# Global blocks as three ordinary steps with weights, placed first in a batch, and the experts' schedule moved

## The chip, the core and the metric

The kernel runs on one core of a Trainium2 chip. The metric is device time in microseconds of one execution; lower is better. The core has TensorE (matmuls; PE in the profile, PEld its weight loads), VectorE (DVE), ScalarE (ACT), GpSimd (POOL) and SyncE (SP, which here only issues transfers). Each runs its own instructions in program order and waits on the others by semaphores.

## What is computed

Block-sparse attention (4 batches, 8 heads, 768 tokens, head size 64, blocks of 32 tokens), then a small expert network on the 128 tokens of each batch with the highest gate score. Cut to what matters:

```python
mask = abs(blk_i - blk_j) <= 1
mask |= (blk_i == 0) | (blk_j == 0) | (blk_i == 23) | (blk_j == 23)
for qb in range(24):
    for kb in sampled_blocks[qb]: mask[qb block, kb block] = True   # 3 drawn key blocks
attn = softmax(where(mask, q @ k.T / 8, -1e9)); x = attn @ v
scores = x @ w_gate                                # per token, x: 768 x 512
top = the 128 tokens of a batch with the highest scores
out[top] = x[top] + sigmoid(scores[top]) * (relu(x[top] @ w1) @ w2)   # w1: 512 x 1024
```

Query blocks 0 and 23 see all 24 key blocks ("global" below); the other 22 see at most eight.

## The kernel before

Tokens are worked in pairs of query blocks, units 0 to 11 of a batch. Unit 0 is the global pair, blocks 0 and 23; the other 11 units are ordinary. Heads are split in two groups g of four (partition halves), and in `ph`, `p2`.

An ordinary unit is one step. `unit_scores` (270) puts the scores of the shared keys and of the gathered ones (`kr`) in two PSUM tiles of the pool `ps_s` (four banks); `maxima` (313) reduces them on VectorE, two instructions; `exps` (328) makes the probabilities on ScalarE, four instructions; `turn` (344) transposes them on TensorE, eight transposes in two banks of `ps_t`, the first evicted by ScalarE and the second by VectorE (`pc`, `pt`); `out_unit` (377) multiplies by v (`vs` shared, `vr` gathered) into the one bank of `ps_o`; `norm` (394) divides by the sums and sends the rows out; `gate` (412) makes the tokens' gate scores in `sps[b]`. `gather` (245) fetches a unit's v rows by indirect DMA on GpSimd and copies its key blocks there, `gather_act` (261) the rest on ScalarE, both three steps ahead.

The global pair takes two steps, `ph` 0 and 1, which stand sixth and seventh among the 13 steps of a batch (`GLOB = 5`, 591). `glob_scores` (297) fills four tiles of 384 columns a step, in two halves; `maxima` takes four reductions and joins the halves; so all 24 key blocks of a row have one maximum. `out_glob` (365) accumulates both steps in one bank, with v of all blocks in `vg` (one 1.6 MB tile, loaded by `load_vg`, 95).

The main loop (640) is written out by hand: iteration s issues prefetches (605), the gather of step s + 3, `norm` and `gate` of s - 1, `turn` of s, `exps` of s + 1, scores of s + 2, the output of s and the maxima of s + 2. Loads are issued on SP in that order. Expert weights: `w_load` (222) and `w_split` (227), one tile of 256 KB in each of steps 1 to 16, split two steps later by ScalarE and VectorE in a high and a low part.

`route` (428) lays out a batch's expert as a plan of (offset, place, piece) counted from the end of its attention (`at`, 421; `run`, 424): `row`, `row_out` and `spread` bring the 768 scores to all partitions over DRAM (for the last batch `on_chip` (451) does it by a matmul with ones); `columns` (463) turns them into columns; six `rank` pieces (483) count on VectorE how many scores are larger; `select` (492), `chosen` (499) and `fetch` (504) fetch the 128 rows by indirect DMA; `xt`, `w1_mm`, `relu`, `ht`, `w2_mm` are the expert (its inputs split in two parts by `split`, 520), `put` (568) the last sum and the scatter. The expert's tiles all come from the one bank of `ps_m` (`mid`, 524). A plan (577 to 585) is 28 steps long: batch 2's runs past the attention, and batch 3's lies behind it.

```python
    plan = [(0, "b", row), (1, "a", row_out), (2, "a", spread)]
plan += [(4, "b", columns), (5, "a", columns_out)]
plan += [(5 + t, "c", lambda t=t: rank(t)) for t in range(6)]
plan += [(11, "a", select), (11, "b", chosen), (12, "a", fetch), (14, "b", xt), (15, "a", xt_out)]
plan += [(15 + i, "b", lambda i=i: w1_mm(0, 4 * i, 4 * i + 4)) for i in range(3)]
plan += [(18, "a", lambda: relu(0)), (18, "b", lambda: ht(0)), (19, "a", lambda: ht_out(0))]
plan += [(19 + i, "b", lambda i=i: w1_mm(1, 4 * i, 4 * i + 4)) for i in range(3)]
plan += [(22, "a", lambda: relu(1)), (22, "b", lambda: ht(1)), (23, "a", lambda: ht_out(1))]
plan += [(23 + i, "b", lambda i=i: w2_mm(6 * i, 6 * i + 6)) for i in range(4)]
```

## Time and profile before

| | us |
|---|---|
| three runs | 355.46, 349.16, 346.52 |
| median | 349.16 |
| the profiled execution | 350.02 |
| its span, first to last instruction | 348.20 |

Times are device time. The profile records one execution; "busy" is time in which an engine worked, "idle before" the pause ahead of an instruction with what ended it. In the program's names, s and gs are scores, mx and gm maxima, pr and gpr probabilities, pt and pc their transposes in PSUM and in SBUF, o and go outputs, h, ht and y the expert's tiles, sb the scores on all partitions, cj the ranks' counts, xe the fetched rows. All operations go through one helper, so every line is L67 and the tiles tell them apart.

### The profile page before, as it was taken

Reading aid. Unit: us, or ns where it says so; the run is one execution under the profiler, and the core shown is the slowest. Engines: PE = TensorE matmul, PEld = TensorE weight load, DVE = VectorE, ACT = ScalarE, POOL = GpSimd, SP = SyncE. Lnnn points to the kernel's source line nnn. Section 1 sums busy time; section 2 is a strip of 40 time slices with the busy share of each in tenths; the row PEclk is TensorE's granted clock in tenths of the full one; section 3 lists DMA queues with packets and bytes.
Section 4 is the critical chain, followed back from the end, with each engine's and each line's share of the span. In section 5 each row is a group of like instructions: output and inputs, shape, how many; then the busy total and the mean of one; then the engine's idle time right before and its main releaser. Section 6 shows DMA issues by size and latency. Waiting matters only on the chain.

```text
span 348.2 us, 13754 instructions
## 1 busy us (share of the span) xinstructions
PE 276.8 (79%) x5508; PEld 206.0 (59%) x5508; DVE 234.7 (67%) x697; ACT 155.6 (45%) x400; POOL 165.9 (48%) x356
## 2 busy tenths in 40 slices
PE   3378789872977878799899988998999968776772
PEld 3266457662754666577567766775677756554551
DVE  4457768774877799997647998677479964761000
ACT  1145658644655665355445553454455531110110
POOL 3688832771770657588426575684165211001001
PEclk9999999997999999899999999999999999887678
DMA  5799886998898749889837597975254312001000
GB/s 212 217 306 332 260 287 184 290 339 236 233 308 266 240 143 311 258 225 293 248 119 235 156 344 214 278 216 167 71 148 118 102 24 86 0 0 60 0 0 30
DMA packets 32038, 65.78 MB, mean 189 GB/s; under 512 B 5736, under 2 KB 12136, under 8 KB 31976
## 3 DMA queue, kind: packets, MB, share of 16 engines
q1 hardware_dynamic: 24296, 39.39, 36.8%
q0 software_dynamic: 7680, 25.53, 24.4%
q8 instruction: 43, 0.70, 0.8%
q14 instruction: 19, 0.16, 0.1%
HBM read 57.55 MB, written 7.35 MB: 186 GB/s over the span
## 4 chain that ended last, share of the span: by engine, by line
PE 44%; DVE 20%; issue 15%; DMA 11%; ACT 5%; POOL 2%; SPq 1%; POOLq 1%; ACTq 0%; DVEq 0%
PE o L67 11%; PE s L67 9%; PE pt L67 7%; PE h L67 5%; DVE mx L67 5%; DMA w<-w 5%; PE y L67 4%; PE gs L67 4%; DVE cj L67 3%; DVE gm L67 3%; ACT pr L67 3%; PE go L67 3%; DMA k<-kt 2%; DVE w_l L67 1%; DVE pc L67 1%
## 5 line engine op out<-in xcount | busy, mean ns | idle before, releaser
L67 POOL DMA_INDIRECT vr<-vt,vidx x88 | 88.0, 1001 | 74.3 <-PE o L67 28.3
L67 DVE TENSOR_REDUCE mx<-s 128x2 f32<-128x512 f32 x88 | 56.5, 682 | 23.7 <-PE s L67 22.2
L67 ACT ACTIVATE pr<-s,mx 128x256 f32<-128x256 f32 x176 | 69.4, 486 | 3.2 <-DVE mx L67 3.2
L67 POOL COPY kr<-k 128x128 f32 (+1 forms) x220 | 63.1, 330 | 4.9 <-PE s L67 4.6
L67 ACT COPY pc<-pt 128x512 f32<-128x512 f32 x44 | 25.7, 585 | 64.5 <-PE pt L67 64.5
L67 PE MATMUL pt<-ident,pr 128*128 128x128 f32 x352 | 50.4, 286 | 1.3 <-DVE ts L67 0.6
L67 PEld LDWEIGHTS pt<-ident,pr 128*128 128x128 f32 x352 | 40.6, 146 | 8.8 <-issue 3.0
L67 PE MATMUL o<-vs,pc 128*64 128x65 f32 x704 | 30.9, 229 | 18.4 <-ACT pr L67 8.6
L67 PEld LDWEIGHTS o<-vs,pc 128*64 128x64 f32 x704 | 25.1, 139 | 31.0 <-ACT pr L67 14.2
L67 PE MATMUL s<-k,q 64*64 64x128 f32 x704 | 31.8, 296 | 9.4 <-DMA vs<-vt 8.1
L67 PE MATMUL s<-kr,q 64*32 64x128 f32 x1408 | 32.0, 286 | 7.0 <-POOL kr L67 3.6
L67 PE MATMUL o<-vr,pc 128*32 128x65 f32 x1408 | 31.0, 225 | 3.3 <-issue 3.3
L67 DVE COPY pc<-pt 128x512 f32<-128x512 f32 x44 | 30.0, 683 | 3.1 <-PE pt L67 2.7
L67 PEld LDWEIGHTS s<-k,q 64*64 64x64 f32 x704 | 20.2, 139 | 17.5 <-DVE q L67 8.4
L67 PEld LDWEIGHTS s<-kr,q 64*32 64x32 f32 x1408 | 19.1, 110 | 16.0 <-issue 11.1
L67 DVE TENSOR_REDUCE gm<-gs 128x1 f32<-128x384 f32 x32 | 16.3, 551 | 16.9 <-PE gs L67 16.9
L67 PE MATMUL y<-w_h,h_hl 128*128 128x512 f32 x64 | 25.1, 451 | 3.0 <-DVE h_hl L67 2.8
L67 ACT COPY kr<-k 128x128 f32 x88 | 22.9, 326 | 10.3 <-DMA vs<-vt 9.8
L67 PEld LDWEIGHTS o<-vr,pc 128*32 128x32 f32 x1408 | 23.1, 111 | 7.0 <-issue 3.9
L67 DVE TENSOR_SCALAR_CACHE_REDUCE cj<-sb,sc 128x128 bf16<-128x128 f32 (+5 forms) x44 | 26.7, 641 | 0.1
L67 PE MATMUL h<-w_h,x_hl 128*128 128x512 f32 x64 | 22.1, 475 | 5.8 <-DVE h_hl L67 3.0
L67 DVE CUSTOM_DVE_ANT_0 j<-x,wg_i 128x256 f32<-128x256 f32 x48 | 22.6, 470 | 0.0
(102 smaller groups left out, 342.2 us busy)
## 6 DMA issues: line engine op xcount, KB each, us to landing
q<-qt SPq DMA_DIRECT2D x16, 384.0 KB
k<-kt SPq DMA_DIRECT2D x16, 384.0 KB
...
vr<-vt,vidx POOLq DMA_INDIRECT x88
```

The lines of the kernel that those rows point to most:

```text
L67: i = getattr(self.engine, name)(*args, **kw)
```

## The change

A batch has 14 steps: the global pair first, as three steps c = 0, 1, 2 of eight key blocks each, then the 11 units. A global step has the form of a unit: two score tiles, two reductions, four exps, eight transposes, 16 output matmuls. Each has its own maxima. `glob_keep` copies the first two outputs (with their sums) out of PSUM on VectorE; `glob_weights` makes the weights exp(own maximum - common maximum); `glob_join` weighs and adds the first two on GpSimd; `glob_last` weighs the third and adds on VectorE; `norm` then divides as before. `vg` comes in three tiles, q's first chunk and the opening's k in parts, in a new order. The maxima of step 0 follow the index arithmetic on VectorE; no gather stands ahead of step 0. Weight tiles are loaded in two of three steps from step 4 on.

In a step in which a piece stands at place "z" (ranks, mostly), ScalarE evicts both transposes. Batches 0 and 1: plan of 24 steps; batch 2 ranks two tiles a step and ends after 19. The last batch: scores of units 0 to 7 are summed four steps before the end of attention, and the first four rank tiles are counted against them in the last two steps; the other third follows behind (`rk` has a fourth column). Its expert tiles, except y, take banks of `ps_s`, and its pieces are interleaved: w1's second half around `ht(0)`, w2's first six around `ht(1)`.

```diff
-WARM = 26
+WARM = 40
...
-    def load_vg(b):
-
-        vg = vgs[b] = inp.tile([P, NB // 4, VR], F32, tag="vg", name=f"vg{b}", bufs=1)
...
+    def load_vg(b, c):
+
+        vg = vgs[b, c] = inp.tile([P, 2, VR], F32, tag="vg", name=f"vg{b}_{c}", bufs=3)
+        r = rows_of(b, 1 + 8 * c)
+        if c < 2:
+            sp.dma_start(vg, vt[r:r + 256].rearrange("(m p) c -> p m c", p=P))
+            return
+        sp.dma_start(vg[:, 0], vt[r:r + 128])
...
-    load_q(0, 0)
-    for c in range(4):
-        load_k(0, 6 * c, 6 * c + 6)
+    load_q(0, 0, 0, 1)
+    load_k(0, 0, 8)
+    load_k(0, 8, 16)
+    load_vg(0, 0)
+    load_k(0, 16, 24)
+    load_q(0, 0, 1, 3)
+    load_vg(0, 1)
     load_vs(0, 1)
-    load_vs(0, 2)
+    load_q(0, 1)
...
+    scale_q(0, 0, 0, 1)
...
-    def glob_scores(b, ph, h):
-        for g in range(G):
-            st[b, "g", ph, g, h] = ps_s.tile([P, 512], F32, tag="s", name=f"gs{b}_{ph}_{g}_{h}")
-        for p2 in range(2):
...
+    def glob_scores(b, c):
+
+        t = [st.setdefault((b, "g", c, g), ps_s.tile([P, 2, 8, BLK], F32, tag="s", name=f"gs{b}_{c}_{g}"))
+             for g in range(G)]
+        for ph in range(2):
+            for p2 in range(2):
+                p = 2 * p2 + ph
+                for g in range(G):
+                    rows = slice(64 * g, 64 * g + 64)
+                    pe.matmul(t[g][64 * p2:64 * p2 + 64, ph], qs[b, 0][rows, 0, p],
+                              ks[b][rows, 8 * c:8 * c + 8, p * BLK:(p + 1) * BLK],
+                              start=ph == 0, stop=ph == 1, tile_position=(64 * g, 64 * p2), skip_group_check=True)
...
+            b, _, c = t
+            if c == 0:
+                gms[b] = small.tile([P, 3, G, 2], F32, tag="gm", name=f"gm{b}", bufs=2)
+            mx = mxs[t] = gms[b][:, c]
...
+        for g in range(G):
+            pr = prs[(*t, g)] = work.tile([P, 512], F32, tag="pr", name=f"pr{tag_of(t)}_{g}", bufs=5)
+            s = st.pop((*t, g)).rearrange("p h k c -> p h (k c)")
+            for ph in range(2):
+                act.activation(pr[:, 256 * ph:256 * ph + 256], s[:, ph], AF.Exp, bias=mx[:, g, ph:ph + 1])
...
+    def turn(t, both):
+
+        pr = [prs.pop((*t, g)) for g in range(G)]
...
-            if c % 8 == 0:
+                c = 256 * (i % 2) + 128 * n
+                pe.transpose(pm[:, i], pr[i // 2][:, c:c + 128], ident)
+            pt = work.tile([P, 4, P], F32, tag="pt", name=f"pc{tag_of(t)}_{n}", bufs=4)
+            if n == 0 or both:
                 act.copy(pt, pm)
             else:
                 vec.tensor_copy(pt, pm)
...
+
+    def glob_weights(b):
+        gm, gw = gms[b], gws.setdefault(b, small.tile([P, 3, NP], F32, tag="gw", name=f"gw{b}", bufs=2))
+        gm = gm.rearrange("p c g h -> p c (g h)")
+        m = small.tile([P, NP], F32, tag="gx", name=f"gx{b}", bufs=2)
+        vec.tensor_tensor(m, gm[:, 0], gm[:, 1], ALU.min)
+        vec.tensor_tensor(m, m, gm[:, 2], ALU.min)
+        vec.tensor_tensor(gw, m.unsqueeze(1).broadcast_to([P, 3, NP]), gm, ALU.subtract)
+        act.activation(gw, gw, AF.Exp)
+
+    def glob_keep(b, c):
+        og = ogs[b, c] = work.tile([P, NP, VW], F32, tag="og", name=f"og{b}_{c}", bufs=2)
+        vec.tensor_copy(og, os_.pop((b, "g", c)))
+
+    def weight(b, c):
+        return gws[b][:, c].unsqueeze(2).broadcast_to([P, NP, VW])
+
+    def glob_join(b):
+        for c in range(2):
+            pool.tensor_tensor(ogs[b, c], ogs[b, c], weight(b, c), ALU.mult)
+        pool.tensor_tensor(ogs[b, 0], ogs[b, 0], ogs[b, 1], ALU.add)
+
+    def glob_last(b):
+        og = ogs.pop((b, 1))
+        vec.tensor_tensor(og, os_.pop((b, "g", 2)), weight(b, 2), ALU.mult)
+        vec.tensor_tensor(og, og, ogs.pop((b, 0)), ALU.add)
+        os_[b, 0] = og
+
+    def out_glob(b, c):
+        o = os_[b, "g", c] = ps_o.tile([P, NP, VW], F32, tag="o", name=f"go{b}_{c}")
+        pt, vg = pts.pop((b, "g", c)), vgs.pop((b, c))
+        for n in range(2):
...
+                    h = p2 * 4 + i
+                    pe.matmul(o[64 * p2:64 * p2 + 64, i], pt[n][:, i, 64 * p2:64 * p2 + 64],
+                              vg[:, n, h * VW:(h + 1) * VW], start=n == 0 and i == 0, stop=n == 1 and i == NP - 1,
+                              tile_position=(0, 64 * p2), skip_group_check=True)
...
-        def on_chip():
-            r = rout.tile([P, FF], F32, tag="hs", name=f"r{b}")[:, 0:S]
-            R["sb"] = rout.tile([P, S], F32, tag="sb", name=f"sb{b}")
...
+        def masked(u0, u1):
+            if "sb" not in R:
+                R["sb"] = rout.tile([P, S], F32, tag="sb", name=f"sb{b}")
+            r = R["r"] = rout.tile([P, 8, 2 * BLK], F32, tag="r", name=f"r{u0}")
+            vec.tensor_tensor(r[:, :u1 - u0], sps[b][:, u0:u1].unsqueeze(2).broadcast_to([P, u1 - u0, 2 * BLK]),
+                              d64.unsqueeze(1).broadcast_to([P, u1 - u0, 2 * BLK]), ALU.mult)
+
+        def sums(u0, u1):
+            R["sbp"] = ps_t.tile([P, 512], F32, tag="t", name=f"sbp{u0}")
+            pe.matmul(R["sbp"][:, :64 * (u1 - u0)], ones, R["r"][:, :u1 - u0].rearrange("p u c -> p (u c)"),
+                      start=True, stop=True)
+
+        def sums_out(u0, u1):
+            act.copy(R["sb"][:, 64 * u0:64 * u1], R["sbp"][:, :64 * (u1 - u0)])
+
+        def columns(t0=0, t1=6):
+            R["scp"] = small_t([P, 6, BLK], f"scp{t0}_")
+            for t in range(t0, t1):
                 pe.transpose(R["scp"][:, t], R["sb"][0:BLK, t * P:(t + 1) * P], ident[0:BLK, 0:BLK])
...
-        def columns_out():
...
+        def columns_out(t0=0, t1=6):
+            if t0 == 0:
+                R["sc"] = rout.tile([P, 6], F32, tag="sc", name=f"sc{b}", bufs=2)
+                R["rk"] = rout.tile([P, 6, 4], F32, tag="rk", name=f"rk{b}", bufs=2)
+                vec.memset(R["rk"], 0.0)
+            vec.tensor_copy(R["sc"][:, t0:t1], R["scp"][:, t0:t1, 0])
...
+        def parts():
+            sc, tb = R["sc"], rout.tile([P, 6, 5], BF16, tag="tb", name=f"tb{b}", bufs=2)
+            R["tb"] = tb
...
-        def rank(t):
-            sb, s, n = R["sb"], R["sc"][:, t:t + 1], t * P
...
+        def rank(t, c0=0, c1=S):
+            sb, s, n, rk = R["sb"], R["sc"][:, t:t + 1], t * P, R["rk"]
+            junk = rout.tile([P, S], BF16, tag="cj", name=f"cj{b}_{t}_{c0}")
+            if c0 < n:
+                vec.tensor_scalar(junk[:, c0:n], sb[:, c0:n], s, 0.0, ALU.is_ge, ALU.add, accum_out=rk[:, t, 0:1])
+            n1 = max(n, c0)
+            i = 3 if c0 > n else 1
+            vec.tensor_scalar(junk[:, n1:c1], sb[:, n1:c1], s, 0.0, ALU.is_gt, ALU.add, accum_out=rk[:, t, i:i + 1])
+            if c0 <= n:
+                vec.scalar_tensor_tensor(junk[:, n:n + P], sb[:, n:n + P], s, before, ALU.is_equal, ALU.mult,
+                                         accum_out=rk[:, t, 2:3])
...
         def mid(name):
+            if last and name != "y":
+                return ps_s.tile([P, 512], F32, tag="s", name=f"{name}{b}")
             return ps_m.tile([P, 512], F32, tag="m", name=f"{name}{b}")
...
+                R["h1", c] = mid(f"h1_{c}")
...
-                pe.matmul(R["h1"], *parts[n], start=n == 0, stop=n == 11)
+                pe.matmul(R["h1", c], *parts[n], start=n == 0, stop=n == 11)
...
         if last:
-            plan = [(0, "b", on_chip)]
+            early = 8
+            plan += [(-4, "z", lambda: masked(0, early)), (-3, "m", lambda: sums(0, early)),
+                     (-3, "z", lambda: sums_out(0, early)), (-2, "m", lambda: columns(0, 4)),
+                     (-2, "z", lambda: columns_out(0, 4))]
+            plan += [(-2 + t // 2, "z", lambda t=t: rank(t, 0, 64 * early)) for t in range(4)]
+            plan += [(0, "z", lambda: masked(early, NU)), (0, "z", lambda: sums(early, NU)),
+                     (0, "z", lambda: sums_out(early, NU)), (1, "n", lambda: columns(4, 6))]
+            plan += [(1, "z", lambda t=t: rank(t, 64 * early, S)) for t in range(4)]
+            plan += [(2, "z", lambda: columns_out(4, 6)), (2, "z", parts), (2, "z", lambda: rank(4)),
+                     (2, "z", lambda: rank(5)), (3, "z", select), (4, "n", chosen), (5, "a", fetch),
+                     (6, "n", xt), (7, "a", xt_out)]
+            w1s(7, 0, 0, 12)
+            plan += [(8, "a", lambda: relu(0))]
+            w1s(8, 1, 0, 8)
+            plan += [(8, "n", lambda: ht(0)), (9, "a", lambda: ht_out(0))]
+            w1s(9, 1, 8, 12)
+            plan += [(10, "a", lambda: relu(1))]
+            w2s(10, 0, 6)
+            plan += [(10, "n", lambda: ht(1)), (11, "a", lambda: ht_out(1))]
+            w2s(11, 6, 24)
+            plan += [(12, "a", put)]
...
-            plan = [(0, "b", row), (1, "a", row_out), (2, "a", spread)]
-        plan += [(4, "b", columns), (5, "a", columns_out)]
-        plan += [(5 + t, "c", lambda t=t: rank(t)) for t in range(6)]
-        plan += [(11, "a", select), (11, "b", chosen), (12, "a", fetch), (14, "b", xt), (15, "a", xt_out)]
-        plan += [(15 + i, "b", lambda i=i: w1_mm(0, 4 * i, 4 * i + 4)) for i in range(3)]
-        plan += [(18, "a", lambda: relu(0)), (18, "b", lambda: ht(0)), (19, "a", lambda: ht_out(0))]
-        plan += [(19 + i, "b", lambda i=i: w1_mm(1, 4 * i, 4 * i + 4)) for i in range(3)]
-        plan += [(22, "a", lambda: relu(1)), (22, "b", lambda: ht(1)), (23, "a", lambda: ht_out(1))]
-        plan += [(23 + i, "b", lambda i=i: w2_mm(6 * i, 6 * i + 6)) for i in range(4)]
-        plan += [(27, "a", put)]
+            fast = b == B - 2
+            plan += [(0, "n", row), (1, "a", row_out), (2, "a", spread), (3, "n", columns), (4, "a", columns_out),
+                     (4, "a", parts)]
+            plan += [(4 + (t // 2 if fast else t), "z", lambda t=t: rank(t)) for t in range(6)]
+            o = 7 if fast else 10
+            plan += [(o, "a", select), (o, "n", chosen), (o + 1, "a", fetch), (o + 2, "n", xt), (o + 3, "a", xt_out)]
+            o += 3
...
+            w1s(o + 1, 0, 6, 12)
+            plan += [(o + 2, "a", lambda: relu(0)), (o + 2, "n", lambda: ht(0)), (o + 3, "a", lambda: ht_out(0))]
+            w1s(o + 3, 1, 0, 6)
+            w1s(o + 4, 1, 6, 12)
+            plan += [(o + 5, "a", lambda: relu(1)), (o + 5, "n", lambda: ht(1)), (o + 6, "a", lambda: ht_out(1))]
+            if fast:
+                w2s(o + 6, 0, 12)
+                w2s(o + 7, 12, 24)
+                plan += [(o + 9, "z", put)]
+            else:
+                for i in range(4):
+                    w2s(o + 6 + i, 6 * i, 6 * i + 6)
+                plan += [(o + 10, "a", put)]
...
-    GLOB = 5
     steps = []
     for b in range(B):
-        units = [(b, u) for u in range(1, NU)]
-        steps += units[:GLOB] + [(b, "g", 0), (b, "g", 1)] + units[GLOB:]
-    n, per = len(steps), NU + 1
...
         b, i = steps[s][0], s % per
-        t = unit_at(s)
+        t = unit_at(s + 1)
         if t:
-            k = inner.index(t) + 3
+            k = inner.index(t) + 2
             if k < len(inner):
                 load_vs(*inner[k])
-        for c, load, scale in ((2, 0, 3), (3, 5, 7), (4, 8, 10), (5, 9, 12)):
-            bq, cq = b + c // 4, c % 4
-            if bq < B and i == load:
-                load_q(bq, cq)
-            if bq < B and i == scale:
-                scale_q(bq, cq)
+        for c, load, scale in ((3, 4, 8), (4, 6, 10), (5, 9, 13), (6, 12, 16)):
+            if i == load and b + c // 4 < B:
+                load_q(b + c // 4, c % 4)
+            bs = b if scale < per else b - 1
+            if i == scale % per and bs >= 0 and bs + c // 4 < B:
+                scale_q(bs + c // 4, c % 4)
         if b + 1 < B:
...
-            if 4 <= i < 8:
-                load_k(b + 1, 6 * (i - 4), 6 * (i - 4) + 6)
-            if i == 9:
-                load_vg(b + 1)
-        if s == 1:
...
+            if i in (5, 7, 8, 10):
+                j = (5, 7, 8, 10).index(i)
+                load_k(b + 1, 6 * j, 6 * j + 6)
+            if i >= 11:
+                load_vg(b + 1, i - 11)
+
+    load_vg(0, 2)
+    load_vs(0, 2)
+    load_q(0, 2)
+    for s in range(2):
+        scores(steps[s])
+        if s:
+            exps(steps[0])
+        maxima(steps[s])
+    route(B - 1, n)
     for s in range(n + 1):
...
+            b, i = steps[s - 1][0], (s - 1) % per
+            done = None if i < 2 else (b, 0) if i == 2 else steps[s - 1]
+            if i < 2:
+                glob_keep(b, i)
+            if i == 0:
+                glob_weights(b)
+            if i == 1:
+                glob_join(b)
+            if i == 2:
+                glob_last(b)
+            if done:
+                norm(*done)
         if s < n:
...
+            turn(steps[s], (s, "z") in due)
...
+            if s + 2 < n:
+                scores(steps[s + 2])
+            run(s, "m")
+            t = steps[s]
             if t[1] == "g":
                 out_glob(t[0], t[2])
             else:
                 out_unit(*t)
...
+            run(s, "n")
             if s + 2 < n:
                 maxima(steps[s + 2])
-            run(s, "c")
-        if 3 <= s:
-            w_split(s - 3)
-        if 1 <= s < 1 + len(ws):
-            w_load(s - 1)
-        if s < n and (s + 1) % per == 0:
+            if s == 0:
+                scale_q(0, 0, 1, 3)
+            if s in (2, 4):
+                scale_q(0, s // 2)
+            run(s, "z")
+        if 6 <= s and (s - 6) % 3 < 2:
+            w_split((s - 6) // 3 * 2 + (s - 6) % 3)
+        if 4 <= s and (s - 4) % 3 < 2:
+            w_load((s - 4) // 3 * 2 + (s - 4) % 3)
+        if s < n and (s + 1) % per == 0 and s + 1 < n:
             route(s // per, s + 1)
     for s, where in sorted(due):
         run(s, where)
```

## Rows read from the trace of the kernel before

**Rows 1.** Stage table: stretch, length, busy PE, PEld, DVE, ACT, POOL, clock, DMA, GB/s.
```profile
0.00:20.13 20.13, 7.30 (x123) 5.50 (x123) 7.65 (x35) 4.55 (x12) 10.63 (x35) 1.00 0.74 223
20.13:87.41 67.28, 52.52 (x1304) 39.43 (x1297) 47.70 (x117) 38.50 (x99) 40.64 (x84) 0.96 0.89 278
87.41:152.59 65.18, 52.72 (x1314) 39.45 (x1310) 55.73 (x165) 36.61 (x96) 39.24 (x83) 0.96 0.81 250
152.59:221.21 68.62, 62.64 (x1372) 46.88 (x1366) 54.86 (x165) 35.75 (x95) 40.74 (x85) 1.00 0.76 232
221.21:287.85 66.64, 60.33 (x1270) 45.09 (x1268) 49.40 (x153) 33.12 (x85) 29.62 (x62) 1.00 0.48 135
165.80:190.45 24.65, 21.97 (x383) 15.10 (x382) 15.13 (x41) 12.60 (x30) 10.48 (x26) 1.00 0.68 206
...
287.85:312.65 24.80, 19.56 (x80) 14.34 (x81) 15.45 (x57) 4.03 (x8) 2.02 (x6) 0.86 0.08 24
...
318.33:341.45 23.12, 18.82 (x56) 13.44 (x56) 1.38 (x2) 2.37 (x4) 0.00 (x0) 0.72 0.00 0
```

**Rows 2.** Chain that ended last, start and us: a unit step, y.
```profile
264.97 0.87 PE pt L67 x8
265.84 1.19 PE s L67 x48
267.04 1.21 PE o L67 x48
268.25 1.13 PE h L67 x4
...
282.91 1.60 PE y L67 x6
```

**Rows 3.** Timeline of ScalarE, batch 0: start, us, instruction, [idle before].
```profile
82.67 0.62 ACT L67 CAST w_h<-w 128x512 fp32r<-128x512 f32 x1 [7.41 <-DMA w<-w]
```

**Rows 4.** Timeline of TensorE, the global steps of batch 2.
```profile
173.25 1.34 PE L67 MATMUL gs<-k,q 64*64 64x384 f32 x8 [1.44 <-ACT gpr L67]
...
179.49 1.25 PE L67 MATMUL pt_g<-ident,gpr 128*128 128x128 f32 x8 [0.68 <-ACT pc_g L67]
```

**Rows 5.** Timeline of VectorE, the opening.
```profile
5.20 0.20 DVE L67 CAST rb<-rb_i 128x72 f32<-128x72 int32 x1 [2.36 <-DMA rb_i<-blocks]
...
11.12 0.55 DVE L67 TENSOR_SCALAR q<-q 128x768 f32<-128x768 f32 x1
...
16.56 1.29 DVE L67 TENSOR_REDUCE mx<-s 128x2 f32<-128x512 f32 x2 [4.89 <-PE s L67]
```

**Rows 6.** Instruction groups: busy us, mean ns, idle before.
```profile
L67 DVE TENSOR_REDUCE mx<-s 128x2 f32<-128x512 f32 x88 | 56.5, 682 | 23.7 <-PE s L67 22.2 <-PE o L67 1.4
...
L67 DVE COPY pc<-pt 128x512 f32<-128x512 f32 x44 | 30.0, 683 | 3.1 <-PE pt L67 2.7
...
L67 DVE TENSOR_TENSOR x<-o,z 128x256 f32<-128x256 f32 x44 | 18.7, 424 | 1.9 <-DVE z L67 0.4
L67 POOL COPY kr<-k 128x256 f32<-128x256 f32 x44 | 17.5, 397 | 0.0
...
L67 DVE TENSOR_SCALAR_CACHE_REDUCE cj<-sb,sc 128x128 bf16<-128x128 f32 (+5 forms) x44 | 26.7, 641 | 0.1
```

**Rows 7.** The gate product: its tile (least, median, most ns) and the timelines.
```profile
L67 DVE CUSTOM_DVE_ANT_0 j<-x,wg_i x48: 413/416/840, 27.2 to 288.8; 128x256 f32<-128x256 f32 x48
...
104.00 0.84 DVE L67 CUSTOM_DVE_ANT_0 j<-x,wg_i 128x256 f32<-128x256 f32 x1
...
103.56 1.54 POOL L67 COPY kr<-k 128x128 f32 x5
```

**Rows 8.** Chain and TensorE's timeline, the end.
```profile
312.65 3.46 DMA xe<-out,it
...
318.34 2.08 PE L67 MATMUL h<-w_h,x_hl 128*128 128x512 f32 x4 [1.46 <-DVE x_hl L67]
```

**Rows 9.** Chain that ended last, after the stall of batch 0.
```profile
85.32 2.16 PE o L67 x48
```

165 lines of the change are left out of this document (38 added, 127 removed).

## The prediction

> **What bounds the kernel now.** I read the stage table first, cut at the starts of the batches' first steps and at the events of the end [rows 1]. The reader is to see three regimes. Batches 2 and 3 are TensorE: 62.64 of 68.62 us and 60.33 of 66.64 us busy at clock 1.00. Batches 0 and 1 are not: 52.5 us of work in 67.3 and 65.2 us, with DMA shares of 0.89 and 0.81. The last 60 us (287.85 to 348.20) are one dependent chain at a clock of 0.86 and then 0.72. The chain of waits then gives the unit step at full clock [rows 2]: eight transposes 0.87, scores 1.19, output 1.21, so 3.3 us, and an expert piece on top (four h matmuls 1.13, six y matmuls 1.60). ScalarE's timeline shows the biggest stall of batch 0: its cast of a weight tile, which stands in order ahead of the probabilities, waited 7.41 us for a load [rows 3]. TensorE's timeline shows the stall of the global blocks [rows 4]: the scores of one global step take all four score banks, so the next ones wait 1.44 us for the exps, and transposes wait 0.68 us for an eviction. That stretch loses 24.65 - 21.97 = 2.7 us [rows 1], and there is one in each batch.
>
> The sum is made against the profiled execution: span 348.20 us, time 350.02 us, so 1.82 us lie around the span. It is 0.9 us above the median of the three runs, well inside their spread.
>
> **The opening.** Before, the first global reduction of scores was at 16.56 and the first transposes at 20.13. VectorE ran its index arithmetic from 5.20, when the block list had landed, to 11.12, scaled q, and only then could TensorE begin; the unit's scores also needed gathered blocks [rows 5]. After, step 0 is a global block, which needs one third of q, eight key blocks and no index. These scores lie beside the index arithmetic. That arithmetic still stands ahead of the maxima on VectorE, and the scaling of q's third now stands ahead of it: 0 to 1.0 us if q lands after the list, taken as 0.4. Maxima at 11.5, and transposes 3.6 later at most (the old distance, 16.56 to 20.13, with another unit's scores between) and 2.5 at least (two reductions of 0.68 and half of four exps, an estimate): 14.0 to 15.1, taken as 14.5. Gain 5.6 us. The 14 more warming matmuls end before the scores are due: nothing. Two more chunks of q and v are ordered on SP ahead of the last third of k: 2.3 MB up to there, 7.4 us at 312 GB/s (278 over its share of 0.89), so k is in before 11.5.
>
> **Global blocks.** Same scores, transposes and outputs in columns, so TensorE's work is unchanged to a few tenths. Two score banks a step instead of four: the waits of [rows 4] go, 2.7 us a batch less what replaces it. Added on VectorE: two evictions and two weighted sums of 128x260, each near the 0.42 us of a 128x256 product [rows 6], and three tiny operations, some 2.1 us; gone are the eight global maxima (six of 0.68 replace them [rows 6], about equal). In a plain step VectorE has 1.36 for maxima, 0.68 for one copy and some 1.2 for that product, the gate product [rows 7] and small ones, 3.3 in all: as much as TensorE's. So I give back 0.6 a batch. On GpSimd three operations of 128x260 are added; no row shows such a two-input operation: below, the 0.40 of the 128x256 copy [rows 6]; above, three times that, 1.2. So 1.2 to 3.6 us a batch. GpSimd is busy 40.6 of 67 us [rows 1] and gathers three steps ahead, so it hides them; if it did not, glob_last on VectorE waits, and behind it the eviction of transposed probabilities and so TensorE. I take 0.
>
> Weighed against a rule: VectorE's gate product with two inputs in SBUF took 0.413 us at least and 0.84 at 104.00, while GpSimd copied blocks from 103.56 on [rows 7]. The Trainium skill, SBUF — State Buffer, section Who interferes with whom, says that a VectorE instruction with two SBUF inputs and a GpSimd instruction that reads SBUF block each other for the whole instruction. By that rule the trace agrees, and the new operations speak against the change (a rival below).
>
> **Batch 0.** Bytes up to 87.41: 20.13 x 223 + 67.28 x 278 = 23.2 MB. After, seven weight tiles instead of twelve or thirteen are loaded in it (about -1.4 MB) and one more q chunk: 22.2 MB. At 312 GB/s that is 71 us, and 2 us of start: a floor of 73. By steps: before, 67.3 less the 7.4 of [rows 3] over 13 steps is 4.6; 14 of them less 2.7 from 14.5 on end at 76.5. The stall of [rows 3] goes because v of the next batch comes in three parts over three steps and the weights two steps in three. I take 76.5 where it was 87.41.
>
> **Batch 1.** 52.72 of work, +2.2 for batch 0's first expert pieces, which come in its last step. Idle was 12.5; I keep 6: the global stall goes, and in the six rank steps the second eviction (0.68) leaves VectorE for ScalarE, whose 36.6 us leave room. 61 instead of 65.2. Its floor by bytes: 16.3 MB and six more weight tiles, 17.9 MB at 312, 57. New here: the scores' columns are transposed one step earlier after the broadcast is issued. If it lands late, TensorE stands and all steps with it: between 0 and the 7.4 us of the late load in [rows 3]; I take 0, inside the idle kept.
>
> **Batch 2.** Work 62.6, +1.6 for one y group now inside, idle 2 instead of 6.0: 66 instead of 68.6.
>
> **Batch 3.** It takes work from the end: 18 h matmuls and transposes of batch 2 with sums and columns (7.2), two more y groups (2.9 to 3.2), less what batch 2 took (3.8): 66.7. Ranks stand twice in a step for batch 2 (three steps) and for the first 512 tokens (two steps): a rank is 26.7 us over 44 instructions plus its third part, some 1.5 [rows 6], so these steps last 5.4 instead of 4.4. With idle, 70 instead of 66.6.
>
> **The end.** Before, from the last unit's output: 24.80 to the fetch, 5.68 until the expert's first matmul, 23.12 for the expert, 6.75 to the end [rows 1]. After, VectorE's 15.45 us of work up to the fetch [rows 1] lose the first parts of four ranks (1.1 each, a full rank of 1.5 less a short one of 0.4) and three operations of 0.7 that are done earlier (batch 1's last sum, two splits of batch 2): 9.0, and some 1.9 of waiting for the sum over partitions and its copy, 10.9. TensorE meanwhile has six h and 24 y of batch 2; the y begin at about 6 and take 6.4 at full clock, more at the lower one; the matmul that picks tokens stands behind them: 13.9 to the fetch. The fetch (3.46 [rows 8]) and what follows stay. The last expert no longer alternates: each eviction has other matmuls beside it, in banks of their own. At full clock 24 h 6.8, 24 y 6.4, transposes 1.0: 14.2. Four h took 2.08 at the lower clock [rows 8]; all so, about 22. In the old end the clock came back during the y, so I take 16.5. Sum 13.9 + 5.7 + 16.5 + 6.75 = 42.9 instead of 60.35.
>
> **Sum.** 76.5 + 61 + 66 + 70 = 273.5, + 42.9 = 316.4, + 1.82: 318 us, 32 below the profiled time. Over half of it (17.5) is the end, 11 the opening and batch 0.
>
> **Rivals.**
> - *The loads bind the first two batches* (DMA share 0.89). The opening's gain and batch 1's are given back, since units only queue behind the same bytes: +11 + 4, 333 us. For it: those shares; against: the rate was higher than the mean in places and bytes fall in batch 0. 0.17.
> - *The stalls go entirely*: batch 0 at 4.0 a step (70.5), batch 1 at its floor (57), the expert near full clock: 306 us. For it: TensorE has only 52.5 of work there. 0.15.
> - *Late broadcast*: columns wait in three batches, 2 to 7.4 us each, 324 to 340. Against: one whole step and more lies between issue and use. 0.05.
> - *Joins block VectorE*: 12 operations of 0.4 to 1.2 us, all on the path: 323 to 332. The blocking seen cost 0.43 a time [rows 7]. 0.04. (The rule of the skill cited above.)
> - *The granted clock falls in the loop.* After the long stall the 48 output matmuls took 2.16 us instead of 1.21 [rows 2, 9]: a step at the lower level costs about 2.7 more. If TensorE's work, spread over three global steps and DMA waits, leaves it idle often enough, 20 steps at the lower level give 318 + 54 = 372. It decides from 12 steps on. Against: with 52.5 us of work in 67 batch 0 still had 0.96. 0.04.
> The forecast keeps 0.55.
>
> **How the numbers follow.** 318 is the likeliest case; unknowns inside it (opening 0.6, clock of the end +5.5 / -2.3, idle in four batches +-6) make 308 to 328. To reach 8 in 10 I take in most of the first two rivals: 303 to 334. Faster by over 2% (under 342) hold all cases but the last and joint failures of the loads and the broadcast: 0.92; within 2%, about what a measurement of this kernel can tell from no change, 0.04; slower by over 2% 0.04.
>
> **What would show it.** Step 0's transposes near 14.5; no ScalarE wait over 3 us for a weight tile; no 1.44 us wait ahead of global scores; the last fetch 13 to 15 us after the last output; a gapless expert of 15 to 18 us after it. Wrong if batch 0 still ends above 84 (loads), if glob_last waits for GpSimd, or if the table shows a clock under 0.9 in a batch.

## The result: 322.6 us, and the profile after

| | before | after |
|---|---|---|
| time, median of 4 runs | 351.74 us (346.52 to 355.46) | 322.62 us (319.40 to 326.86) |
| profiled execution, span | 350.02, 348.2 us | 326.86, 325.2 us |

The ratio is 0.924, with a 95% interval of 0.909 to 0.940: faster, by 29 us from median to median and by 26 by the ratio. The forecast was 318, with a range of 303 to 334. Ratios, here and below, compare mean times without the profiled execution and without any that is over 1.5% above the fastest of the rest, so they are not the quotients of the medians beside them, which are over all executions. The profiled execution of the changed kernel is the longest of its four, 4.2 us above their median (that of c_after below is 3.4 above its own); so lengths of stages are checked below against its kin, and what only it shows is not explained.

The stage table of the changed kernel: stretch, length, busy time of PE, PEld, DVE, ACT and POOL, then granted clock, DMA share and GB/s. The stretches are the opening, the four batches, last output to fetch, fetch to the expert's first product, expert, end; they answer to [rows 1].

```profile
0.00:13.13 13.13, 6.31 (x72) 5.09 (x73) 7.16 (x36) 2.10 (x4) 3.78 (x21) 0.94 0.78 272
13.13:73.27 60.14, 53.06 (x1312) 40.48 (x1312) 47.47 (x116) 37.33 (x102) 47.70 (x96) 0.93 0.95 289
73.27:139.68 66.41, 55.86 (x1343) 43.10 (x1337) 58.31 (x170) 41.27 (x110) 46.11 (x91) 0.92 0.92 280
139.68:210.62 70.94, 65.13 (x1388) 50.54 (x1387) 55.78 (x165) 39.41 (x106) 42.64 (x87) 0.95 0.78 224
210.62:281.98 71.36, 64.70 (x1372) 50.38 (x1370) 53.45 (x169) 39.34 (x105) 32.41 (x67) 0.98 0.48 131
281.98:298.41 16.43, 13.09 (x56) 9.63 (x50) 10.39 (x46) 1.63 (x4) 0.80 (x4) 0.79 0.07 15
298.41:303.59 5.18, 1.12 (x4) 0.72 (x4) 0.98 (x4) 0.62 (x2) 2.00 (x2) 0.81 0.32 101
303.59:318.40 14.81, 14.79 (x56) 11.21 (x56) 2.06 (x3) 2.37 (x4) 0.00 (x0) 0.83 0.00 0
318.40:325.20 6.80, 0.00 (x0) 0.00 (x0) 0.75 (x1) 0.00 (x0) 0.98 (x1) 0.78 0.10 39
```

The time came from both ends: the opening is 7.0 us shorter, batch 0 7.1, the end 17.1 (43.22 instead of 60.35). Batches 1 to 3 gave 8.3 of it back: they are 1.2, 2.3 and 4.7 us longer. The last expert is gapless, 14.79 of 14.81 us busy.

VectorE's timeline in the opening, against [rows 5]:

```profile
5.18 0.29 DVE L67 TENSOR_SCALAR q<-q 128x256 f32<-128x256 f32 x1 [4.17 <-DMA q<-qt]
...
11.80 2.48 DVE L67 TENSOR_REDUCE gm<-gs 128x2 f32<-128x512 f32 x4
```

The first maxima start at 11.80 instead of 16.56, straight behind the index arithmetic, and the first transposes are only 1.33 later, not 3.6.

ScalarE's timeline, the casts of weight tiles, where before had the 7.41 us of [rows 3], and the groups of the joins (busy, mean ns, idle before), with the gate product's tile (least, median, most ns) that answers to [rows 7]:

```profile
143.99 0.62 ACT L67 CAST w_h<-w 128x512 fp32r<-128x512 f32 x1 [1.23 <-DMA w<-w]
```

```profile
L67 POOL TENSOR_TENSOR og<-og,gw 128x260 f32<-128x260 f32 x8 | 4.9, 617 | 30.0 <-ACT gw L67 19.0 <-DVE og L67 11.0
L67 POOL TENSOR_TENSOR og<-og,og 128x260 f32<-128x260 f32 x4 | 3.0, 738 | 0.3
L67 DVE COPY og<-go 128x260 f32<-128x260 f32 x8 | 3.3, 414 | 0.0
L67 DVE TENSOR_TENSOR og<-go,gw 128x260 f32<-128x260 f32 x4 | 1.7, 422 | 0.0
```

```profile
L67 DVE CUSTOM_DVE_ANT_0 j<-x,wg_i x48: 414/425/637, 28.6 to 284.4; 128x256 f32<-128x256 f32 x48
```

The one wait of ScalarE for a weight over 1 us is 1.23 us (c_after, the same kernel again, has two, of 2.71 and 1.46). GpSimd waits for its join's operands (30 us of idle before them), and no row of VectorE's waits names GpSimd: the joins are hidden.

Now what the forecast did not have. The timeline of TensorE in batch 1 around the step that selects tokens, and VectorE's in the same step:

```profile
118.72 0.67 PE L67 MATMUL s<-k,q 64*64 64x128 f32 x16
119.32 0.67 PE L67 MATMUL s<-kr,q 64*32 64x128 f32 x32
122.49 0.69 PE L67 MATMUL o<-vs,pc 128*64 128x65 f32 x16 [2.50 <-issue]
...
125.60 1.08 PE L67 MATMUL pt<-ident,pr 128*128 128x128 f32 x4 [0.90 <-DVE ts L67]
126.61 1.13 PE L67 MATMUL s<-k,q 64*64 64x128 f32 x16
```

```profile
119.59 1.81 DVE L67 TENSOR_SCALAR sel<-slot,rs 128x128 bf16<-128x128 bf16 x6
...
121.96 0.42 DVE L67 TENSOR_TENSOR x<-o,z 128x256 f32<-128x256 f32 x1 [0.29 <-DVE z L67]
```

The output at 122.49 writes the bank that x reads on VectorE until 122.38, and x stands there behind the selection's six operations. The page calls the 2.50 us "issue"; going by the two engines' times it is VectorE's order. Here the next unit's scores took 1.13 instead of 0.67: the clock has fallen. The same step and the next in a stage table:

```profile
117.70:123.87 6.17, 3.67 (x115) 2.93 (x111) 5.78 (x22) 2.96 (x8) 3.32 (x7) 1.00 0.91 295
123.87:130.80 6.93, 6.03 (x111) 4.32 (x107) 5.36 (x17) 2.65 (x7) 4.53 (x8) 0.52 0.84 242
```

After the pause a step's work takes 6.03 us of TensorE at a granted 0.52 (the lower level) instead of 3.67 at 1.00 in the step before.

Other pauses stand in the middle of a group on one tile, where the products just before had already used the same tiles:

```profile
39.10 0.66 PE L67 MATMUL o<-vr,pc 128*32 128x65 f32 x31
41.84 0.24 PE L67 MATMUL o<-vr,pc 128*32 128x65 f32 x1 [2.07 <-issue]
...
48.01 0.65 PE L67 MATMUL s<-k,q 64*64 64x128 f32 x12
50.34 0.44 PE L67 MATMUL s<-k,q 64*64 64x128 f32 x4 [1.67 <-issue]
55.41 0.45 PE L67 MATMUL s<-kr,q 64*32 64x128 f32 x15 [0.77 <-issue]
```

From the pause at 41.84 to that at 50.34 there are 1 + 8 + 48 + 48 + 8 + 12 = 125 products, to the next one 4 + 32 + 48 + 8 + 16 + 17 = 125.

### The profile page after: what moved, and what is told of

The parts are those of the page before. It is cut to its first block, busy times and chain, and to the rows that moved or that the text cites. A ratio compares the mean times of both kernels' runs of the same rounds, so it can differ in the third digit from the quotient of the medians.

```text
span 325.2 us, 13953 instructions
## 1 busy us (share of the span) xinstructions
PE 274.1 (84%) x5586; PEld 211.2 (65%) x5586; DVE 236.4 (73%) x704; ACT 164.1 (50%) x435; POOL 176.4 (54%) x368
## 4 chain that ended last, share of the span: by engine, by line
PE 51%; DVE 15%; issue 14%; DMA 11%; ACT 5%; ACTq 1%; SPq 0%; POOLq 0%; POOL 0%; DVEq 0%
PE o L67 12%; PE s L67 11%; PE pt L67 9%; DMA w<-w 5%; PE y L67 4%; PE h L67 4%; DVE cj L67 3%; PE go L67 3%; PE pt_g L67 3%; DMA out<-x 2%; PE gs L67 2%; DVE mx L67 2%; ACT pr L67 2%; DMA k<-kt 2%; DVE x L67 1%
## 5 line engine op out<-in xcount | busy, mean ns | idle before, releaser
L67 POOL DMA_INDIRECT vr<-vt,vidx x88 | 88.1, 1001 | 54.4 <-PE o L67 18.6
L67 ACT COPY pc<-pt 128x512 f32<-128x512 f32 x63 | 35.2, 588 | 63.1 <-PE pt L67 63.1
L67 POOL COPY kr<-k 128x128 f32 (+1 forms) x220 | 66.2, 341 | 0.3
L67 PE MATMUL o<-vs,pc 128*64 128x65 f32 x704 | 31.8, 232 | 19.3 <-issue 10.4
L67 PEld LDWEIGHTS o<-vs,pc 128*64 128x64 f32 x704 | 25.8, 141 | 30.7 <-issue 12.2
L67 PE MATMUL o<-vr,pc 128*32 128x65 f32 x1408 | 32.0, 229 | 4.4 <-issue 3.3
L67 PEld LDWEIGHTS o<-vr,pc 128*32 128x32 f32 x1408 | 23.8, 113 | 8.3 <-issue 4.0
L67 DVE TENSOR_SCALAR_CACHE_REDUCE cj<-sb,sc 128x256 bf16<-128x256 f32 (+5 forms) x48 | 27.7, 607 | 1.7 <-ACT sb L67 1.3
L67 PEld LDWEIGHTS s<-k,q 64*64 64x64 f32 x704 | 20.1, 139 | 9.9 <-issue 9.6
L67 ACT ACTIVATE pr_g<-gs,gm 128x256 f32<-128x256 f32 x48 | 18.9, 484 | 10.2 <-DVE gm L67 10.2
L67 POOL TENSOR_TENSOR og<-og,gw 128x260 f32<-128x260 f32 x8 | 4.9, 617 | 30.0 <-ACT gw L67 19.0
L67 PE MATMUL h<-w_h,x_hl 128*128 128x512 f32 x64 | 19.7, 433 | 1.6 <-issue 0.9
```

The source lines that it names most:

```text
L67: i = getattr(self.engine, name)(*args, **kw)
```

## The experiments

The stages of all profiles, in us, cut as above (end: from the last unit's output). Each row is a stage table; the forecast's is its sum.

| | opening | batch 0 | 1 | 2 | 3 | end | span |
|---|---|---|---|---|---|---|---|
| before | 20.1 | 67.3 | 65.2 | 68.6 | 66.6 | 60.4 | 348.2 |
| forecast | 14.5 | 62.0 | 61 | 66 | 70 | 42.9 | 316.4 |
| after | 13.1 | 60.1 | 66.4 | 70.9 | 71.4 | 43.2 | 325.2 |
| c_after (again) | 12.8 | 62.1 | 70.5 | 66.4 | 71.2 | 41.2 | 324.1 |
| e1 globals alone | 12.7 | 59.3 | 61.9 | 65.5 | 63.7 | 58.9 | 322.0 |
| e4 one weight load | 13.1 | 58.1 | 62.0 | 65.3 | 69.8 | 41.4 | 309.6 |
| e5 evictions on VectorE | 13.0 | 61.6 | 65.3 | 69.2 | 71.1 | 42.5 | 322.6 |
| e6 single ranks | 12.7 | 60.8 | 65.7 | 68.4 | 64.3 | 43.3 | 315.2 |
| e7 old plan, new expert | 13.2 | 59.0 | 64.8 | 67.4 | 64.0 | 49.9 | 318.2 |
| e8 both undone | 12.7 | 61.3 | 66.6 | 66.5 | 65.7 | 41.3 | 314.2 |
| e9 weights every step | 12.8 | 63.3 | 67.8 | 66.8 | 69.9 | 41.2 | 321.9 |
| e10 few loads | 12.8 | 59.4 | 61.8 | 66.3 | 71.4 | 43.4 | 315.2 |
| e11 hybrid | 13.3 | 60.4 | 59.4 | 66.4 | 67.6 | 43.4 | 310.4 |

**c_after.** The changed kernel again.

> The changed kernel as it is, as the partner of the next three on the same chip. Its first profile showed batch 1 at 66.4 us and batch 2 at 70.9 us, each some 5 over the forecast. Theory A (the loads and TensorE's own instruction stream hold batches 0 and 1; the stretches vary from run to run): 318 to 325 us with the same table of stages within 3 us a batch. Theory B (the new order of expert pieces holds them): the same time, but batches 1 and 2 exactly as long as in the first profile.

322.47 us (316.48 to 326.82, four runs), ratio 0.9125 [0.8986, 0.9263], where before took 350.38. The time is theory A's, its 3 us a batch are not: batches 1 and 2 changed places (70.5 and 66.4 for 66.4 and 70.9), so one profile's batch is known to some 4 us. Their sum is 137 in both, but that is no measure of its noise: e1 and e7 below have the same instructions in these two batches and 127.4 and 132.2, at granted clocks of 1.00 and 1.00 against 0.95 and 0.97.

**e1, one half.** The global blocks, loads and opening of after, the old 28-step plan:

```diff
-            early = 8
...
-            fast = b == B - 2
...
+        if last:
+            plan = [(0, "n", on_chip)]
+        else:
+            plan = [(0, "n", row), (1, "a", row_out), (2, "a", spread)]
+        plan += [(4, "n", columns), (5, "a", columns_out), (5, "a", parts)]
...
+        plan += [(27, "a", put)]
```

> Global blocks as three steps first, loads and opening as changed, but every batch's expert by the old plan of 28 steps (scores of the last batch summed at the end, all ranks at the end, one bank for the expert). Theory A: opening and batch 0 as in the changed kernel (13 and 60 us), batches 1 and 2 within 2 us of it, the end again about 60 us; batch 3 some 4 us shorter: 333 to 338 us. Theory B: batches 1 and 2 some 5 us shorter each, as forecast for the globals: 324 to 328 us.

326.0 us (323.7 to 327.1), ratio 0.937 [0.928, 0.947]: theory B's number. Its stage table:

```profile
72.06:133.93 61.87, 50.04 (x1333) 38.55 (x1327) 55.96 (x166) 40.76 (x109) 39.14 (x79) 1.00 0.91 274
133.93:199.39 65.46, 62.61 (x1392) 48.40 (x1387) 55.18 (x164) 39.35 (x106) 40.20 (x81) 1.00 0.81 245
199.39:263.08 63.69, 60.14 (x1357) 47.17 (x1356) 51.34 (x155) 37.37 (x101) 42.89 (x88) 1.00 0.60 165
263.08:322.00 58.92, 37.00 (x136) 26.29 (x136) 18.68 (x63) 6.96 (x13) 3.79 (x7) 0.83 0.07 21
```

The end is the old one (58.9), and yet the kernel is 24 us faster than before: opening 7.4, batch 0 8.0, and some 3 us in each of the other three. On top of this half the new schedule took 16 to 18 us from the end. All but 3.5 of them by the medians, all but 8.6 by the ratios of e1 and c_after, went back into the batches.

One of the places is the step that selects tokens in batch 2. TensorE's timeline there, in after and then in e1:

```profile
193.42 1.14 PE L67 MATMUL o<-vs,pc 128*64 128x65 f32 x16 [3.00 <-issue]
```

```profile
188.25 0.69 PE L67 MATMUL o<-vs,pc 128*64 128x65 f32 x16
```

The wait is there in all eight profiles with the new schedule on the new global steps (2.71 to 3.00 us), and in none of e1, e7 and e11, which keep the old plan in this batch. In their selecting step and the steps around it stand six y products each of an earlier batch; the new plan has done those before. That they are what hides the wait is inferred from this.

**e2, the other half.** The old global blocks, loads and opening under the new plan, both evictions on ScalarE in steps with ranks.

```diff
-        plan += [(5 + t, "c", lambda t=t: rank(t)) for t in range(6)]
...
+            plan += [(4 + (t // 2 if fast else t), "z", lambda t=t: rank(t)) for t in range(6)]
...
+            turn(steps[s], (s, "z") in due)
```

> The old global steps, loads and opening, with the changed plan for all experts, the ranks in two parts and the second eviction on ScalarE in rank steps. Theory A: opening and batch 0 as before (20 and 67 us), batches 1 and 2 as before within 2 us, batch 3 longer by 4, the end 43 instead of 60: 335 to 341 us. Theory B: batches 1 and 2 longer by 3 to 5 each than before: 344 to 350 us.

356.3 us (354.1 to 359.6), ratio 1.026 [1.014, 1.039]: slower than before (whether by more than 2% is open), outside both expectations. The end is 41.7 us, 18.6 shorter, but batches 1 to 3 take 6.8, 4.3 and 13.0 more (from one batch's row of sums to the next, and from the last one to the last output). TensorE's timeline in two of its global steps:

```profile
121.42 1.62 PE L67 MATMUL go<-vg,pc_g 128*64 128x65 f32 x48 [2.77 <-DVE x L67]
...
265.39 1.88 PE L67 MATMUL go<-vg,pc_g 128*64 128x65 f32 x48 [3.54 <-DVE x L67]
```

There the products wait for VectorE, 9.5 us in four waits; before has one such wait, of 1.22 us. So the new schedule pays only on the new global steps: -24 and +6 alone, -28 together by the medians (-22, +9 and -30 by the ratios). Which of its edits costs most on the old steps wasn't tried.

**e4, the weight loads.** One tile stands for all 16.

```diff
-            stage[i] = work.tile([P, DM], F32, tag="f", name=f"w{i}", bufs=2)
-            sp.dma_start(stage[i], ws[i][2])
+            if "w" not in stage:
+                stage["w"] = const.tile([P, DM], F32, name="w_one")
+                sp.dma_start(stage["w"], ws[i][2])
+            stage[i] = stage["w"]
```

> The changed kernel with one weight tile loaded once and split 16 times, so 3.9 of 65.8 MB are not moved (the expert computes with that one tile in place of w1 and w2). Theory A (transfers hold batches 0 and 1): 3.9 MB at 290 GB/s are 13 us, of which 6 to 12 show: 310 to 316 us, and TensorE's pauses in the middle of a group of matmuls (issue, 13.7 us in all) fall under 9. Theory B: under 3 us, 318 to 322, pauses unchanged.

314.55 us (311.28 to 319.88), ratio 0.901 [0.889, 0.913]: theory A by its time. It is 8 us under c_after's median on the same chip, but 4 by the ratios, whose intervals overlap. The other clause of theory A missed: the row that it means, output products put down to issue, is 12.0 us where after has 13.7, not under 9. Batches 1 and 2 take 62.0 and 65.3, near the forecast's 61 and 66:

```profile
71.16:133.18 62.02, 52.76 (x1343) 41.14 (x1337) 57.97 (x170) 41.43 (x110) 43.44 (x88) 0.97 0.82 251
133.18:198.46 65.28, 61.53 (x1388) 48.19 (x1387) 55.22 (x164) 39.36 (x106) 43.60 (x90) 1.00 0.79 239
```

TensorE is busy 114.3 us in the two, where after has 121.0 and c_after 121.5 for the same products. So some 7 of the 10 us between these profiles are work at the lower level of the clock. Why that level lasts longer with the loads is not shown: the pauses of the selecting steps are as long here (2.97 and 2.71 us).

**e5, e6, e8: what the schedule gave back.** e5 sets `turn(steps[s], False)`, e6 sets `fast = False`, e8 does both.

> The changed kernel, but in the steps with ranks VectorE again makes the second of the two evictions of turned weights (0.68 us each) instead of ScalarE. In the profiles so far batches 1 and 2 together take 137 us in the changed kernel, 127 with the old 28-step plan on the new globals. Theory A: the second eviction fills ScalarE, so that the copies of the weight tiles come late, their two buffers hold SyncE's queue, and the loads behind come late: batches 1 and 2 fall to 127 to 130 and the time to 312 to 316. Theory B: their length comes from TensorE's pauses in the middle of a group of products (0.5 to 3 us each, every 125 products or so) and the low clock after them, whoever evicts: batches 1 and 2 stay at 135 to 140, and the time at 320 to 326.

325.07 us (323.25 to 325.84), ratio 0.931 [0.925, 0.937]: theory B by its time, with 134.5 us for batches 1 and 2. Who evicts is not what lengthens them. Nor are theory B's pauses inside a group: those of 0.4 us and more come to 0.65 us in these two batches, to 2.6 in after, 1.8 in c_after and 3.1 in before, and e9 has none there and takes 134.6 us.

> The changed kernel, but the second last batch has one rank a step as the others, not two, and its expert comes three steps later, after the last unit's output. Theory A: two ranks a step make the three steps of batch 3 that hold them 6.8, 5.6 and 8.6 us, against 5.3, 4.4 and 4.4 with one: batch 3 falls from 71 to 64 or 65 us, and the expert that moves behind the last output lies beside the last ranks for the most part (0 to 3 us more): 316 to 319. Theory B: those three steps are long through the expert's products and the early ranks of the last batch, not through the pairs: batch 3 stays at 69 or more, the end grows by 3 to 5, and the time is 323 to 327.

316.42 us (315.72 to 319.69), ratio 0.9085 [0.9005, 0.9165]: theory A. Batch 3 and the end:

```profile
207.59:271.89 64.30, 59.57 (x1356) 46.65 (x1354) 51.96 (x165) 39.95 (x106) 33.33 (x67) 1.00 0.52 144
271.89:315.20 43.31, 30.73 (x126) 23.23 (x126) 14.81 (x54) 5.79 (x11) 3.79 (x7) 0.84 0.07 24
```

Batch 3 is 7 us shorter, and the end is 43.3 as with the pairs, though twelve more h products and four more transposes lie in it. The pairs bought nothing. TensorE's timeline there shows why:

```profile
282.70 1.91 PE L67 MATMUL h<-w_h,x_hl 128*128 128x512 f32 x4
284.41 0.35 PE L67 MATMUL selp<-tb,sel 128*128 128x5 bf16 x6
```

The product that picks tokens comes 12.5 us after the last output (284.41 - 271.89), in after 15.5 (297.45 - 281.98), where 24 y products stand ahead of it:

```profile
297.45 0.31 PE L67 MATMUL selp<-tb,sel 128*128 128x5 bf16 x6
```

> The changed kernel with both edits: second evictions on VectorE and one rank a step in the second last batch. Theory A: both gains add up, 8 and 5 us: 307 to 312. Theory B: neither gives anything: 320 to 327. A third outcome, 314 to 318, means that one of them carries it and the runs with one edit say which.

321.64 us (315.98 to 324.62), ratio 0.924 [0.917, 0.931]: theory B by its number, and no better than e6 alone. By its stages it is not theory B: batch 3 is again short (65.7). But the profiled execution is the shortest of its runs (315.98 us, the others 321.02 to 324.62); where the longer ones lose their time is open.

**e7, one piece of the new end.** e1, with the last expert in interleaved pieces and score banks:

```diff
+            if last and name != "y":
+                return ps_s.tile([P, 512], F32, tag="s", name=f"{name}{b}")
...
+        if last:
+            w1s(15, 0, 0, 12)
+            plan += [(16, "a", lambda: relu(0))]
+            w1s(16, 1, 0, 8)
...
+            w2s(19, 6, 24)
```

> The kernel of e1 (new global steps, loads and opening, old 28-step plan), and of the new end only the last expert: its pieces interleaved and in banks of their own; no early ranks, no pairs, no second eviction on ScalarE. Theory A: from the fetched rows to the end it takes 22.7 us instead of 31.9, nothing else changes: 326.0 less 9.2, 315 to 319. Theory B: the last expert is bound by its products at the lower clock and the pieces only fill idle time of one engine: less than 4 us, 322 to 325.

(One clause of it is wrong: in steps with ranks e1 and e7 do keep the second eviction on ScalarE.) 319.68 us (318.94 to 321.71), ratio 0.917 [0.911, 0.923], 6.3 under e1's median and near theory A. The end is 49.9 instead of 58.9, so the pieces give 9 us of the 16 to 18. The other 7 to 9 come with the early ranks and what else the new end has; that wasn't tried alone.

**e9, the spacing of the weights.**

```diff
-        if 4 <= s and (s - 4) % 3 < 2:
-            w_load((s - 4) // 3 * 2 + (s - 4) % 3)
+        if 1 <= s < 1 + len(ws):
+            w_load(s - 1)
```

> The changed kernel with the old spacing of the 16 weight loads: one a step from the second step on, split two steps later, instead of two in three steps from the fifth on. Theory A (the prediction's): the spacing is what removed ScalarE's wait of 7.4 us for a weight tile in batch 0; with the old one that wait, or one like it, is back, batch 0 takes 66 to 68 us instead of 60 to 62 and batch 1 stays at 66 to 70: 327 to 331. Theory B: the bytes only move from batch 1 to batch 0: batch 0 gets 5 to 8 us longer and batch 1 as much shorter: 319 to 325.

325.02 us (320.28 to 328.08): theory B's upper edge, but batch 0 got only some 2 us longer, and batch 1 no shorter. It is 2.5 above the changed kernel's medians, less than these runs can tell. The wait itself is back, half as long, and in batch 1 (from 76.12). Its chain that ended last:

```profile
69.49 5.60 DMA w<-w
...
75.15 7.58 DMA w<-w
...
84.27 1.12 PE pt_g L67 x4
```

Two weight loads follow each other up to 82.73, ScalarE waits 3.49 us for the second, and TensorE stands 3.85 us before 84.27.

**e10, most loads left out.**

```diff
         i = vs_of(b, u)
+        if vs_b[i] is not None and vs_b[i] >= 0:
+            return
```

> The changed kernel with most of its loads left out in the loop: one weight tile is loaded and stands for all 16, and the direct rows of the values are loaded for the first five units and stand for all later units. Queries, keys, the gathered keys and values and all arithmetic stay. Theory A: batches 0 to 2 are held by the loads, and TensorE's pauses inside a group of products are long only where the DMA engines are full: the pauses fall from 17 to 20 us to under 9 in sum, batch 0 to 53 to 56 and batch 1 to 58 to 60 us: 300 to 308. Theory B: the pauses come at the same rate whatever is loaded, and the order of the engines' work holds the batches: pauses of 11 us or more, and 311 to 316, as with the one weight load alone.

317.13 us, one execution, outside both expectations. TensorE's pauses inside a group (0.4 us and more) fell to 4.6 us in sum, all in batch 0, where after has 9.0, c_after 10.2, before 8.7 and the other runs with all loads, e12 apart, 6.7 to 9.1; e4 has 4.9. So the pauses get shorter in sum with fewer loads, as theory A has it. But batches 1 and 2 take 61.8 and 66.3 where e4 has 62.0 and 65.3: they don't get shorter than with the weights alone left out (theory B). With the loads out of the way the page also names the wait of the selecting step:

```profile
119.14 0.69 PE L67 MATMUL o<-vs,pc 128*64 128x65 f32 x16 [3.01 <-DVE x L67]
```

Waits for x make up 5.8 of TensorE's 10.4 us of idle in batch 1 and 2.8 of 3.4 in batch 2.

**e11, the pieces that paid.** Single ranks, the old plan for batches 0 and 1, a weight load every second step:

```diff
+        elif b < B - 2:
+            plan = [(0, "n", row), (1, "a", row_out), (2, "a", spread)]
+            plan += [(4, "n", columns), (5, "a", columns_out), (5, "a", parts)]
...
+            fast = False
...
+        if 3 <= s and s % 2:
+            w_load((s - 3) // 2)
```

> What paid in the runs so far, put together: the changed kernel with one rank a step in the second last batch, the first two batches on the old 28-step plan, and a weight load every second step. Theory A: the terms of the separate runs add up: opening 12.8, batches 59, 63, 66.5 and 64.5, end 43, and 1.8 around the span: 308 to 313, under the 316.4 of the run with single ranks alone. Theory B: the length of batches 0 to 2 is set by what the loads move in all, and neither the later weights nor the spread experts change it: 314 to 319.

310.29 us (307.70 to 312.06), ratio 0.882 [0.874, 0.890]: theory A, and faster than both kernels. The sum fits in part by luck: batch 1 is 3.6 us under its term and batch 3 3.1 above it. Batch 1 shows the gain best:

```profile
73.64:132.99 59.35, 50.18 (x1334) 38.73 (x1327) 53.97 (x163) 39.62 (x107) 37.98 (x79) 1.00 0.90 277
```

Seven us less than after, of which 5.7 are TensorE's busy time (50.18 for 55.86). Of these, ten products that the old plan leaves to batch 2 are about 2.2, the forecast's term for them; the rest is the clock, which stayed at 1.00.

**e12, the selection later**, behind the maxima of its step (e11's plan, first two batches):

```diff
-            plan += [(11, "a", select), (11, "n", chosen), (12, "a", fetch), (14, "n", xt), (15, "a", xt_out)]
+            plan += [(11, "z", select), (12, "n", chosen), (13, "a", fetch), (14, "n", xt), (15, "a", xt_out)]
```

> The kernel of e11, and for the first two batches the selection (six operations of VectorE, some 1.8 us) is moved from the start of step 11, ahead of that step's normalisation, to its end, behind the maxima; the products with it and the fetch come one step later. Theory A: the pauses of 2 to 3 us before an output group in the step of the selection come from VectorE, which reads the previous output out of its bank only behind the selection: steps 11 of batches 1 and 2 get 1.5 to 2.5 us shorter and nothing else longer: 305 to 308 where e11 had 310.3. Theory B: the pause is TensorE's supply of instructions, as the page's word for it (issue) suggests, or the work is only late one step further on: no change, 309 to 312.

341.01 us, where before took 368.15 on this chip instead of 350: ratio 0.929 [0.924, 0.935]. Neither expectation can be judged by its number, as e11 did not run on this chip. Its ratio is higher than e11's 0.882, and TensorE's pauses are of another kind there: 24 of 0.4 us and more inside groups, 15 us in sum, in batch 0 for the most part 103 to 105 products apart. The steps with the products that pick tokens took 4.4 and 4.9 us, in e11 5.4 and 5.2. In batch 1 this stands ahead of the output, where e11 has 1.68 us; in batch 2 neither has a pause over 0.2 us:

```profile
138.42 0.69 PE L67 MATMUL o<-vs,pc 128*64 128x65 f32 x16 [0.86 <-ACT pr L67]
```

The pause halved, then; whether time was gained stays open.

## Why the forecast was right, and where it was not

The sum of the spans, 316.4, missed the profiled 325.2 by 8.8: opening -1.4, batch 0 -1.9, batch 1 +5.4, batch 2 +4.9, batch 3 +1.4, end +0.3. Against the median the miss is 4.6. The step that failed is the idle kept in batches 1 and 2; the other stages held within 2 us. That the total came as near is in part luck: 3.2 us too much in the opening and batch 0 stand against 10.3 too little in these two batches.

- *Opening, 14.5: 13.1.* Maxima at 11.80 as worked out (11.5). The distance to the transposes was sized too long: the lower bound counted two reductions and half of four exps (2.3 us by these terms, not 2.5), and it was 1.33 us.
- *Global blocks: right.* The waits of 1.44 us before global scores are gone. GpSimd's operations took 0.617 and 0.738 us, inside the bounds of 0.40 and 1.2, hidden as taken. The joins held VectorE up nowhere: in after and c_after all twelve ran beside copies and reductions out of PSUM only, which kept their usual 0.68 to 0.69 us. The gate product did meet GpSimd's copies of key blocks, as in before: in after it took 0.414 to 0.468 us in the 25 cases with no copy or arithmetic of GpSimd beside it, and up to 0.637 in the other 23 (0.84 in before [rows 7]). The rule of the Trainium skill, SBUF — State Buffer, section Who interferes with whom, is that a VectorE instruction with two SBUF inputs contends with a GpSimd instruction that reads SBUF. The trace agrees with it for the copies; for the joins it is not tried, as none met such an instruction.
- *Batch 0, 62.0: 60.1 (58 to 63 in the other runs of the table).* The wait of 7.41 us went (at most 1.23 in after, 2.71 in c_after). That the spacing of the weights did it is borne out in part: with the old spacing a wait of 3.5 us is back (e9), but in batch 1, and what it costs is less than these runs can tell.
- *Batch 1, 61, and batch 2, 66: 66.4 and 70.9.* Together that is 137 us instead of 127; the other profiles with all loads and the new plan have 133 to 137. The work was forecast well (54.9 and 64.2 us; measured 55.9 and 65.1, in c_after 58.2 and 63.3), the idle was not. "Idle was 12.5; I keep 6" became 10.5 (12.2 in c_after), and "idle 2" became 5.8 (3.2). The waits of the global steps went, but others stand in their place. The largest is that of the selecting steps, 2.5 and 3.0 us, where the output waits until VectorE has read the previous one; in e10, where the page names such waits, they come to 5.8 and 2.8 us in sum. VectorE's work in batch 1 was not added up: it is busy 58.3 us there, 55.7 before. The numbers of e4 (62.0 and 65.3) come near the forecast in part by luck: its idle in batch 1 is 9.3 us, and its work is less than forecast. So the rival *the loads bind* was true in part, at 8 us by the medians or 4 by the ratios (e4), not 15; and the rival *the clock falls* at a few steps, not 12. The floor by bytes was the wrong place to look: it allowed 57 us.
- *Second evictions on ScalarE*, for which idle was taken away in batch 1: worth nothing that these runs can tell (e5).
- *Columns one step earlier, taken as 0*: in after TensorE waits 0.89 us ahead of them, in c_after 2.00, and no row of either names the broadcast. Both waits end 1.6 to 1.7 us after a block of instructions landed (last section), so they are not shown to be the price of the columns. e2 has one wait for it, of 2.59 us.
- *Batch 3, 70: 71.4.* Right, and priced as work taken from the end. That this work had to be taken was not asked: single ranks take 64.3 with the same end (e6).
- *End, 42.9: 43.2.* Fetch at 16.43 (13.9 taken): the y products began at 7.3, not 6, and ran 8.2 us, partly at the lower level, not 6.4, and token picking stands behind them. The expert, 14.8, came out under its 16.5. So the sum fits because misses cancel. e7 shows the gapless pieces as cause of half the gain.
- *"Over half of it (17.5) is the end"*: the size is right, the account is not. Measured alone, the first half of the change carries 24 of 28 us by the medians (22 of 30 by the ratios), since the schedule pays for its shorter end in batches 1 to 3.
